# A fused attention, gated MLP and soft mixture-of-experts kernel: another tail, other slot logits, new step orders

## The chip, the cores and the metric

The kernel runs on one core of a Trainium2 chip. The metric is the device time of one launch in microseconds (us). In the words below PE is TensorE (PEld its weight loads), DVE is VectorE, ACT is ScalarE, POOL is GpSimd and SP is SyncE, whose queue issues nearly all DMAs. PSUM is the memory that PE writes its products to; DVE and ACT copy them out of it.

## What is computed

Three stages in a row, float32 in and out:

```python
# 1 attention: 4 batches, 12 heads, 448 rows, head width 64
q_n, k_n = rmsnorm(q, g_q), rmsnorm(k, g_k)
attn = softmax(q_n @ k_n.T / 8) @ v          # gathered to x: 1792 x 768
# 2 gated MLP: w_gate, w_val 768 x 1536, w_out 1536 x 768
x = (silu(x @ w_gate) * (x @ w_val)) @ w_out
# 3 soft mixture: phi 768 x 32, 8 experts with 4 slots each, w1 8 x 768 x 1024, w2 8 x 1024 x 768
logits = x @ phi                             # 1792 x 32
slot_input = softmax(logits, axis=0).T @ x   # 32 x 768
slot_out[e] = relu(slot_input[e] @ w1[e]) @ w2[e]
out = softmax(logits, axis=1) @ slot_out     # 1792 x 768
```

## The kernel before, in words

**Units of work.** The program is one long list of steps `t`, written out in Python. In the first 28 steps (`step0`, t below `M0`) PE does the attention of batch 0, one quarter of a head pair per step, and beside it the 12 blocks of `w_out` are multiplied with `phi` (tiles `wot`, `wpp`, `wpq`, `wp`). From t = 28 on (`step`) each step also multiplies one block of gate or value weights with a batch of `x` (`gv`, L615: 36 products of 128x128 by 128x448 into the tile `pg`); 24 such blocks make a batch, 96 all four. The attention of batches 1 to 3 runs beside them until t = 95. Weights and `x` are split in a rounded part and a rest (`wh`, `wl`, `xh`, `xl`; type fp32r) and multiplied in three terms.

**Orders.** Which piece of a step stands before which is set by lists of names: `ORDA`, `ORD0` and `ORDB` for t below 2, below 24 and below 28, `ORD1` for the batch 0 blocks and `ORD2` for the others. Every engine executes its own instructions in that order. Some of the names: `S` scores, `M0`/`M1` row maxima (DVE), `E0`/`E1` exponentials (ACT), `P0`/`P1` transposes of the probabilities (PE, tile `tp`), `V0`/`V1` their copies (tile `pt`), `X` probabilities times v, `T`/`TP` transposes of q and k, `G0`/`G1` the two halves of `gv`, `HT` transposes of the MLP's hidden rows (`th`), `LG` partial logits (`lp`), `NB` the transposed inverse sums (`rb`), `R` the integer part of a weight conversion (ACT or POOL, tiles `hpos`, `hneg`).

**Slots.** After a batch's 24 blocks come `Z1` to `Z4`. `slots1` sums the partial logits to `lt`, 128 x 448, each slot repeated four times, and multiplies the same logits once more into their transposed form `ln` (L703; in the last batch L705 too, since its last hidden block is not in the sum yet). `slots2` takes maximum and exponential and copies `ln` to `ce`, which the last stage's softmax over slots starts from. `slots3` transposes the exponentials (`dp`), DVE copies them to `dn`, and `slots4` multiplies the hidden rows with them (`sp`). In the last batch `slots4_last` adds the scaled sums of the other batches (`acl`, `wp`) and multiplies by `w_out` (`sip`).

**Experts and tail.** The expert weights (28 units of 1.5 MB) come through 15 buffers; a load is issued when the buffer's last reader is done. PE multiplies slots with w1 (L1431) and w2 (L1458, tile `so`, four column strips side by side). The last four units are the halves of the last two experts' w2, so that output columns 0 to 383 are ready before the others. `slot_out` (L1403 to L1407) then copies two 32-row strips of `so` into the zeroed tile `sos`, lays them over one another with a product by the 0/1 matrix `sel`, and splits that in rounded part and rest; `output` (L1417 to L1422) makes one 112 x 384 block of the output with one fp32r product of depth 96 from it and from `ct`, which holds the combine weights, their rest and the weights again. DVE and ACT copy the blocks out in turn and SP stores them in pairs. `TO` says how many of the 16 blocks of the first half stand after each of the last three units, `TF` and `LF` how many filler products (`fill`, L115, tile `warm_ps`) stand at given places.

Of the kernel before, what the change touches and what calls it, by code (L numbers as in the profile page):

```python
# [21 lines left out]
def attn_moe_softmoe_kernel(  # L22
# [15 lines left out]
    nc = tc.nc  # L38
# [649 lines left out]
    def slots1(b):  # L688

        d = bt[b]  # L690
        lg = d["lg"]
        d["lt"] = pt_tile("lt")
        n = NS * d["n"]
        ht = d["ht"].pop(KF - 1, None)
        one = ht is None
        nc.tensor.matmul(d["lt"][:, :S], stack[:n].rearrange("p j s -> p (j s)"), lg, start=True, stop=one)
        if not one:
            nc.tensor.matmul(d["lt"][:, :S], d["wp4"].rearrange("p j s -> p (j s)"), ht, start=False, stop=True)
            h_trans(B * NU - 1, ht)
        ln = pt_tile("ln")  # L700
        for c in range(NC):
            o, cs = ln[:CP, NS * c : NS * c + NS], slice(CP * c, CP * c + CP)
            nc.tensor.matmul(o, lg[:, cs], stack[:n, 0, :], start=True, stop=one)  # L703
            if not one:
                nc.tensor.matmul(o, ht[:, cs], wp[:, KF - 1, :], start=False, stop=True)  # L705
        d["ln"] = ln

    def slots2(b):
# [12 lines left out]
        nc.vector.tensor_copy(out=ce[:, b], in_=d.pop("ln")[:CP, : NC * NS].rearrange("p (c s) -> p c s", c=NC))  # L721
# [8 lines left out]
        d["et"] = et  # L730

    def slots3(b):
        d = bt[b]
        dp = pt_tile("dp")
        for c in range(NC):
            nc.tensor.transpose(
                dp[:CP, NS * c : NS * c + NS], d["et"][:NS, CP * c : CP * c + CP], ident[:NS, :NS]
            )
        d["dn"] = mp.tile([CP, NC, NS], F32, tag="dn", name="dn", bufs=1)
        nc.vector.tensor_copy(out=d["dn"], in_=dp[:CP, : NC * NS].rearrange("p (c s) -> p c s", c=NC))  # L740
# [75 lines left out]
    def acc_scale():  # L816
        accl.append(mp.tile([P, S], F32, tag="lg", name="acl", bufs=1))
        accl.append(wp.rearrange("p f s -> p (f s)"))
        accl.extend([ht_tile("acl", n) for n in (1, 0)])
        for g in range(NG):  # L820
            for r, o in acc_parts(g):
                nc.scalar.activation(out=o, in_=accp[g][:, r], func=AF.Copy, scale=bt[B - 1]["sml"][:, 3:4])
# [246 lines left out]
    def step(t):  # L1069
# [210 lines left out]
        "CT M0 M1 E0 E1 S X R P0 V0 P1 V1 NA NB TP TH SS WT WV U C WE NC XM U2 TL Q XH W2 XL G2"  # L1280
# [4 lines left out]
    ORDB = (  # L1285
        "M1 TP CT NA WT TH NB WV E1 M0 P1 P0 E0 X S R V1 U2 TL NC V0 U XM XH WE XL C G2 Q SS W2"
# [73 lines left out]
    with tc.manual_schedule():  # L1360
# [31 lines left out]
        sel = stack.rearrange("p j s -> p (j s)")[:, : 3 * NS]  # L1392
        sst = [None, None]

        def slot_out(n):

            if n == 0:
                t = unit_tile(NE + B).bitcast(F32R)
                sst[:] = [t[: 3 * NS, 384 * i : 384 * i + 384] for i in range(2)]
            r, cs = slice(2 * NS * n, 2 * NS * (n + 1)), slice(384 * n, 384 * n + 384)  # L1400
# [115 lines left out]
```

## Time and profile before

| what | us |
|---|---|
| median of 3 runs | 833.52 (832.75 to 835.16) |
| the profiled execution, own time | 833.85 |
| its span, first to last instruction | 832.1 |
| PE busy | 790.9 (95%) |
| DVE, ACT, POOL busy | 462.1, 439.3, 333.1 |

The page of the profile gives for each engine its busy time, and in 40 slices how busy it was and what TensorE clock was granted. The other views are answers of the same trace: busy times in chosen stretches, who waited for whom, the chain of waits that ended last in order of time, and the instructions in order of time. Matmuls are pipelined there and their ends are modelled, so the times of neighbours overlap.

### The profile page before, as it was taken

Reading aid. Unit: us, or ns where it says so; the run is one execution under the profiler, and the core shown is the slowest. Engines: PE = TensorE matmul, PEld = TensorE weight load, DVE = VectorE, ACT = ScalarE, POOL = GpSimd, SP = SyncE. Lnnn points to the kernel's source line nnn. Section 1 sums busy time; section 2 is a strip of 40 time slices with the busy share of each in tenths; the row PEclk is TensorE's granted clock in tenths of the full one; section 3 lists DMA queues with packets and bytes.
Section 4 is the critical chain, followed back from the end, with each engine's and each line's share of the span. In section 5 each row is a group of like instructions: output and inputs, shape, how many; then the busy total and the mean of one; then the engine's idle time right before and its main releaser. Section 6 shows DMA issues by size and latency. Waiting matters only on the chain.

```text
span 832.1 us, 14229 instructions
## 1 busy us (share of the span) xinstructions
PE 790.9 (95%) x5460; PEld 594.0 (71%) x5460; DVE 462.1 (56%) x777; ACT 439.3 (53%) x940; POOL 333.1 (40%) x327
## 2 busy tenths in 40 slices
PE   6799989999999999999999999999999999988685
PEld 5556657778778767787778677877878888555353
DVE  4879978777778555555556555545354344220013
ACT  3777877878678546556566455655333333220012
POOL 7987867675756543445444344322000000010000
PEclk8999999999999999999999999999999999999877
DMA  6566665765656312322223222221337778899997
GB/s 212 161 197 188 204 206 164 238 223 177 195 188 223 107 53 80 110 91 77 83 80 95 68 85 60 69 75 52 96 107 252 285 286 321 270 397 403 403 343 235
DMA packets 77891, 148.87 MB, mean 179 GB/s; under 512 B 5888, under 2 KB 48128, under 8 KB 77824
## 3 DMA queue, kind: packets, MB, share of 16 engines
q1 hardware_dynamic: 77824, 147.97, 53.5%
q8 instruction: 43, 0.70, 0.3%
q14 instruction: 24, 0.20, 0.1%
HBM read 128.29 MB, written 19.66 MB: 178 GB/s over the span
## 4 chain that ended last, share of the span: by engine, by line
PE 60%; DMA 6%; ACT 1%; POOL 1%; DVE 1%; issue 0%; SPq 0%; DVEq 0%; ACTq 0%; POOLq 0%
PE pg L615 33%; DMA w<-in_moe_w_dram 6%; PE tp L521 5%; PE xp L548 5%; PE s L442 3%; PE th L659 2%; PE so L1458 2%; PE sp L746 1%; PE lp L679 1%; PE tq L372 1%; PE s L446 1%; PE s L1417 1%; PE s L1431 1%; PE sip L800 0%; POOL pr L486 0%; PE ln L703 0%
## 5 line engine op out<-in xcount | busy, mean ns | idle before, releaser
L615 PE MATMUL pg<-xh,wh 128*128 128x448 f32 x576 | 222.5, 386 | 0.0
L615 PE MATMUL pg<-xl,wh 128*128 128x448 f32 x576 | 210.6, 366 | 0.0
L615 PE MATMUL pg<-xh,wl 128*128 128x448 f32 x432 | 157.9, 365 | 0.1
L457 DVE TENSOR_REDUCE sm<-s 128x1 f32<-128x448 f32 x168 | 100.5, 617 | 73.4 <-PE s L442 52.7
L469 ACT ACTIVATE pr<-s,sm 128x448 f32<-128x448 f32 x168 | 106.2, 639 | 63.5 <-DVE sm L457 61.1
L486 POOL TENSOR_SCALAR pr<-pr,su 128x448 f32<-128x448 f32 x84 | 70.9, 854 | 117.5 <-DVE su L482 106.0
L615 PEld LDWEIGHTS pg<-xh,wh 128*128 128x128 f32 x576 | 108.6, 189 | 12.4 <-issue 5.1
L615 PEld LDWEIGHTS pg<-xl,wh 128*128 128x128 f32 x576 | 108.9, 189 | 6.4
L521 PE MATMUL tp<-ident,pr 128*112 128x128 f32 x672 | 101.9, 280 | 4.3 <-ACT pt L535 2.1
L521 PEld LDWEIGHTS tp<-ident,pr 128*112 128x112 f32 x672 | 74.7, 135 | 38.2 <-issue 13.2
L231 ACT CAST wh<-raw 128x768 fp32r<-128x768 f32 x96 | 79.5, 830 | 29.0 <-PE pg L615 22.8
L239 DVE TENSOR_TENSOR wl<-raw,wh 128x768 fp32r<-128x768 f32 x72 | 81.0, 1124 | 11.2 <-ACT wh L231 11.2
L615 PEld LDWEIGHTS pg<-xh,wl 128*128 128x128 f32 x432 | 81.2, 188 | 7.2 <-DVE wl L239 0.5
L535 ACT COPY pt<-tp 112x512 f32<-112x512 f32 x130 | 74.0, 595 | 13.3 <-PE tp L521 7.4
L341 POOL TENSOR_TENSOR ri<-ss,mhalf 112x16 f32<-112x16 f32 (+1 forms) x25 | 70.1, 2805 | 2.1
L423 POOL CAST qz<-qa 64x128 fp32r<-64x128 f32 x48 | 35.1, 732 | 78.3 <-DVE qa L414 70.1
L442 PE MATMUL s<-ka,qa 64*128 64x448 f32 x432 | 63.6, 399 | 0.8 <-ACT qa L403 0.7
L660 ACT COPY hn<-th 112x512 f32<-112x512 f32 x48 | 28.4, 591 | 58.9 <-PE th L659 58.9
L548 PE MATMUL xp<-pt,vt 112*64 112x448 f32 x288 | 58.1, 546 | 0.0
L347 POOL TENSOR_TENSOR qn<-qk,ri 112x512 f32<-112x512 f32 x46 | 52.9, 1150 | 1.1
L615 PE MATMUL pg<-xh,raw 128*128 128x448 f32 x144 | 52.6, 366 | 0.0
L197 POOL TENSOR_SCALAR hpos<-r 128x768 uint16<-128x768 int16 x36 | 46.2, 1282 | 4.6 <-DMA r<-in_moe_w_gate_dram 1.7
(161 smaller groups left out, 1103.9 us busy)
## 6 DMA issues: line engine op xcount, KB each, us to landing
w<-in_moe_w_dram SPq DMA_DIRECT2D x25, 1536.0 KB, 10.6
raw<-w SPq DMA_DIRECT2D x72, 384.0 KB, 3.2
w<-raw SPq DMA_DIRECT2D x36, 384.0 KB, 2.9
r<-in_moe_w_out_dram SPq DMA_DIRECT2D x12, 768.0 KB, 5.1
r<-in_moe_w_gate_dram SPq DMA_DIRECT2D x12, 768.0 KB, 5.2
r<-in_moe_w_val_dram SPq DMA_DIRECT2D x12, 768.0 KB, 5.0
qk<-in_q_dram SPq DMA_DIRECT2D x24, 224.0 KB, 3.2
qk<-in_k_dram SPq DMA_DIRECT2D x24, 224.0 KB, 3.4
```

The costliest lines, as they stand in the source:

```text
L231: (nc.vector.tensor_copy if u - NO < NU and WH1 == "v" else nc.scalar.copy)(out=wh, in_=wst[u]["raw"])
L239: eng.tensor_tensor(out=wl, in0=wst[u]["raw"], in1=wst[u]["wh"].bitcast(F32), op=ALU.subtract)
L341: nc.gpsimd.tensor_tensor(out=ri, in0=ss, in1=mhalf[:, : len(ns)], op=ALU.pow)
L347: eng.tensor_tensor(out=st[i]["qn"][:, n].rearrange("p c h d -> p h c d"), in0=st[i]["qk"][:, n], in1=st[i]["ri"][:, n] .rearrange("p (h c ...
L442: nc.tensor.matmul(sc[j], qa[r, wt, c * P : (c + 1) * P], ka[r, mv, :], start=(n == 0), stop=(n == 2))
L457: nc.vector.tensor_reduce(out=d["sm"][:, j : j + 1], in_=d["sc"][j], axis=AX.X, op=ALU.max, negate=True)
L469: nc.scalar.activation(out=p, in_=d["sc"][j], func=AF.Exp, bias=d["sm"][:, j : j + 1], accum_out=st[i]["su"][:, c, j : j + 1])
L486: nc.gpsimd.tensor_scalar(out=p, in0=p, scalar1=su[:, j : j + 1], scalar2=1.0, op0=ALU.mult, op1=ALU.mult)
L521: nc.tensor.transpose(tp[:CP, ck * P : (ck + 1) * P], pr[:, ck * CP : (ck + 1) * CP], ident)
L535: eng(out=st[i]["pt"][j][:, :, c * P : (c + 1) * P], in_=tp)
L548: nc.tensor.matmul(xp[HD * j : HD * j + HD, :S], d["vt"][:, j, ck, :], d["pt"][j][:, ck, :], start=(ck == 0), stop=(ck == NC - 1),)
L615: nc.tensor.matmul(d[r], wt[:, P * c : P * c + P], mv, start=(c == 0 and n == 0), stop=(c == KD - 1 and n == 2),)
```

## The change

Five things change.

1. `slots1` no longer makes `ln`. `slots2` copies the first 32 rows of `lt` to `lr` (the space of `lg`), and `slots3` transposes `lr` beside the exponentials and copies it to `ce`, on DVE, in the last batch on ACT.
2. In the last batch the 12 filler products ahead of `slots1` go (`LF`, in fours), and the sums are kept in other tiles (`accl`).
3. The tail's products are in full float32, of depth 32: `ct` holds four equal copies of the combine weights, one for each strip of rows, `slot_out` is one copy of 64 rows, and a block takes two products of 192 columns, one from each strip, into two PSUM tiles; DVE copies the first, ACT the second. `sel`, the split and the zeroing are gone.
4. `TO` puts all 16 blocks of the first half ahead of the products of the last two units, and `TF` (in fours too) drops the tail's fillers, 16 products in each of two places.
5. All five order lists are new.

```diff
@@ slots1
-        ln = pt_tile("ln")
-        for c in range(NC):
-            o, cs = ln[:CP, NS * c : NS * c + NS], slice(CP * c, CP * c + CP)
-            nc.tensor.matmul(o, lg[:, cs], stack[:n, 0, :], start=True, stop=one)
-            if not one:
-                nc.tensor.matmul(o, ht[:, cs], wp[:, KF - 1, :], start=False, stop=True)
-        d["ln"] = ln
@@ slots2
-        nc.vector.tensor_copy(out=ce[:, b], in_=d.pop("ln")[:CP, : NC * NS].rearrange("p (c s) -> p c s", c=NC))
...
+        d["lr"] = d["lg"][:NS]
+        (nc.vector.tensor_copy if LRE == "v" else nc.scalar.copy)(out=d["lr"], in_=lt[:NS, :S])
@@ slots3
+        for n, (src, dst) in enumerate(((d["et"], d["dn"]), (d["lr"], ce[:, b]))):
+            o = dp[:CP, NC * NS * n : NC * NS * (n + 1)]
+            for c in range(NC):
+                nc.tensor.transpose(o[:, NS * c : NS * c + NS], src[:NS, CP * c : CP * c + CP], ident[:NS, :NS])
+            if n == 0 or b < B - 1:
+                nc.vector.tensor_copy(out=dst, in_=o.rearrange("p (c s) -> p c s", c=NC))
+            else:
+                nc.scalar.copy(out=dst, in_=o.rearrange("p (c s) -> p c s", c=NC))
@@ combine2, combine3: four copies of the weights for three, one ACT copy for ACT's cast and DVE's rest
-        cb = ct[:, S * b : S * b + S]
-        evac_hi(cb, cp[: 3 * NS, :S])
-        sub_lo(cb[NS : 2 * NS], cp[NS : 2 * NS, :S], cb[NS : 2 * NS])
+        nc.scalar.copy(out=ct[:, S * b : S * b + S], in_=cp[:, :S])
@@ the lists (ORD1, ORD2, ORDA and ORDB are new in the same way)
-    LF = [4, 3, 2, 3]
+    LF = [4, 3, 2, 0]
+    LRE = 'v'
-    TF, TO = [0, 0, 0, 0, 4, 4, 0], [0, 8, 16, 16]
+    TF, TO = [0, 0, 0, 0, 0, 0, 0], [0, 16, 16, 16]
-        "M1 X TP M0 P0 R NA SS WT NB TH S U2 TL V0 WV P1 NC XM U CT C W2 XH E0 E1 V1 WE Q XL G2"
+        "X TP P0 M0 WT NB M1 R SS TH NA V0 S U2 P1 NC XM U WV CT TL E0 XH C V1 XL W2 G2 E1 Q WE"
@@ slot_out
-            for j in (2 * n, 2 * n + 1):
-                eng = nc.scalar.copy if j % 2 else nc.vector.tensor_copy
-                eng(out=sos[NS * j : NS * j + NS, DQ * j : DQ * j + DQ], in_=so[NS * j : NS * j + NS, :])
-            s3 = pt_tile("s3")
-            nc.tensor.matmul(s3[: 3 * NS, :384], sel[r], sos[r, cs], start=True, stop=True)
             fill(TF[5 + n])
-            nc.scalar.copy(out=sst[n], in_=s3[: 3 * NS, :384])
-            sub_lo(sst[n][2 * NS :], s3[2 * NS : 3 * NS, :384], sst[n][2 * NS :])
+            (nc.scalar.copy if n else nc.vector.tensor_copy)(out=sos[r], in_=so[r, :])
@@ output
-            op = (s_tile(i % 5) if i % 5 < 3 else pt_tile("op"))[:CP, :384]
-            nc.tensor.matmul(op, ct[:, S * b + CP * c : S * b + CP * c + CP], sst[n], start=True, stop=True)
-            eng = nc.scalar.copy if c % 2 else nc.vector.tensor_copy
-            eng(out=ot[b][:, c, cs], in_=op)
+            ops = [(s_tile(k) if k < 3 else pt_tile("op"))[:CP, :DQ] for k in ((2 * i + j) % 6 for j in range(2))]
+            for j in range(2):
+                r = slice(NS * (2 * n + j), NS * (2 * n + j + 1))
+                nc.tensor.matmul(
+                    ops[j], ct[r, S * b + CP * c : S * b + CP * c + CP], sos[r], start=True, stop=True
+                )
+            for j, eng in enumerate((nc.vector.tensor_copy, nc.scalar.copy)):
+                eng(out=ot[b][:, c, DQ * (2 * n + j) : DQ * (2 * n + j + 1)], in_=ops[j])
```

How the instructions stand at three places follows; a row is line, operation, output and inputs, and size.

PE in the tail before, from the eighth output block to the products of the last unit (`s` and `op` are blocks of the output, by the PSUM tile that they go to):

```order
L1417 MATMUL s<-w,ct 112x384 x3
L1458 MATMUL so<-w,h1m 32x192 x16
L1417 MATMUL op<-w,ct 112x384 x2
L1417 MATMUL s<-w,ct 112x384 x3
L1417 MATMUL op<-w,ct 112x384 x2
L1417 MATMUL s<-w,ct 112x384
L1458 MATMUL so<-w,h1m 32x192 x16
```

and PE of the change, the end of the same stretch:

```order
L1404 MATMUL s<-sos,ct 112x192 x3
L1404 MATMUL op<-sos,ct 112x192 x3
L1404 MATMUL s<-sos,ct 112x192 x2
L1447 MATMUL so<-w,h1m 32x192 x32
L1404 MATMUL s<-sos,ct 112x192 x3
```

The products of the last two units (`so`, two times 16) moved behind the whole first half, whose 16 blocks are now 32 products of half the width.

DVE in the last batch's slots before, from the maximum of `lt` to the first sum for `sip`:

```order
L716 TENSOR_REDUCE sml<-lt 128x1
L720 TENSOR_TENSOR mrun<-mrun,sml 128x1
L721 COPY ce<-ln 112x128
L727 SCALAR_TENSOR_TENSOR ssum<-ssum,sml 128x1
L740 COPY dn<-dp 112x128
L784 TENSOR_TENSOR acl<-acl,sp 128x384
```

and in the change:

```order
L709 TENSOR_REDUCE sml<-lt 128x1
L713 TENSOR_TENSOR mrun<-mrun,sml 128x1
L719 SCALAR_TENSOR_TENSOR ssum<-ssum,sml 128x1
L724 COPY lg<-lt 32x448
L736 COPY dn<-dp 112x128
L782 TENSOR_TENSOR wp<-wp,sp 128x384
```

The copy from `ln` ahead of `ssum` is gone, and a copy of 32x448 logits stands ahead of the copy to `dn` instead.

PE at the slots of the second batch before (`pg` is `G0`, one row of its nine shown at each end):

```order
L736 MATMUL dp<-ident,et 112x32 x4
L521 MATMUL tp<-ident,pr 112x128 x4
L615 MATMUL pg<-xh,wh 128x448
...
L615 MATMUL pg<-xh,wl 128x448
L746 MATMUL sp<-hn,dn 32x512 x12
```

and in the change:

```order
L442 MATMUL s<-ka,qa 128x448 x6
L734 MATMUL dp<-ident,et 112x32 x4
L734 MATMUL dp<-ident,lg 112x32 x4
L744 MATMUL sp<-hn,dn 32x512 x12
L521 MATMUL tp<-ident,pr 112x128 x4
```

The `sp` products, which read DVE's copy `dn` of the first transposes, stood behind nine `pg` products and now follow the transposes directly. Over the whole list PE's `pg` products, cut in 137 runs before, are cut in 160: 23 of the runs of 18 became two runs of 9 with transposes between them, and 19 of the 23 runs of 8 `tp` transposes became two of 4.

## Rows read from the trace of the kernel before

**Rows 1.** Busy us by stretch (PE, PEld, DVE, ACT, POOL), granted clock, DMA share, GB/s.

```profile
125.00:700.00 575.00, 574.35 (x3360) 454.85 (x3358) 338.70 (x550) 328.68 (x673) 227.98 (x215) 1.00 0.42 138
740.00:780.00 40.00, 34.03 (x622) 20.46 (x614) 5.55 (x18) 4.11 (x10) 4.02 (x11) 1.00 1.03 403
```

**Rows 2.** Waits of PE, 20 to 130 us: total us, times, longest.

```profile
PE tp L521 <- ACT pt L535: 2.1, 1, 2.1
...
PE rb L505 <- ACT pt L535: 1.3, 1, 1.3
...
PE warm_ps L115 <- ACT pr L469: 0.2, 1, 0.2
```

**Rows 3.** Busy us as in rows 1, 12 to 48 us.

```profile
12.00:48.00 36.00, 26.88 (x197) 18.39 (x198) 24.30 (x39) 22.20 (x54) 33.83 (x33) 0.91 0.61 189
```

**Rows 4.** Chain of waits in order of time: start us, us, what; around 280 us.

```profile
276.75 1.06 PE tp L521 x8
277.81 3.67 PE pg L615 x18
...
288.24 0.58 PE tp L521 x4
288.82 1.84 PE pg L615 x9
290.65 0.44 PE th L659 x4
```

**Rows 5.** Chain of waits, slots of the third and the last batch.

```profile
613.66 0.75 PE lt L696 x2
614.41 0.72 PE ln L703 x8
...
617.04 0.33 PE dp L736 x4
...
711.92 0.69 PE warm_ps L115 x12
```

**Rows 6.** Instructions in order of time: start, us, [idle before]; last batch's slots.

```profile
708.12 0.61 DVE L685 TENSOR_TENSOR lg<-lp,lg 32x448 f32<-32x448 f32 x1 [3.33 <-PE lp L679]
...
715.46 0.64 ACT L724 ACTIVATE et<-lt,mrun 128x448 f32<-128x448 f32 x1
...
718.46 0.29 DVE L740 COPY dn<-dp 112x128 f32<-112x128 f32 x1 [0.58 <-PE dp L736]
...
719.23 4.08 PE L746 MATMUL sp<-hn,dn 112*32 112x512 f32 x24
```

**Rows 7.** Waits of SP's queue, 715 to 740 us.

```profile
SPq L906 <- PE sp L746: 10.2, 2, 8.9
```

**Rows 8.** Instructions in order of time, tail.

```profile
804.22 0.34 DVE L1403 COPY sos<-so 32x192 f32<-32x192 f32 x1 [6.93 <-PE so L1458]
...
808.10 19.58 SPq L1422 DMA_DIRECT2D out_dram<-w  x18
...
813.57 2.79 PE L1458 MATMUL so<-w,h1m 128*32 128x192 f32 x32
...
819.33 0.78 PE L1417 MATMUL s<-w,ct 96*112 96x384 f32 x3 [1.15 <-DVE w L62]
...
819.80 1.02 DVE L1419 COPY w<-s 112x384 f32<-112x384 f32 x2 [0.52 <-PE s L1417]
```

**Rows 9.** Busy us as in rows 1; around the last slots and in the tail.

```profile
720.00:722.00 2.00, 2.00 (x16) 0.57 (x12) 0.69 (x2) 0.00 (x0) 0.00 (x0) 0.53 0.12 40
...
807.00:809.00 2.00, 1.95 (x10) 1.29 (x12) 1.48 (x4) 1.26 (x3) 0.00 (x0) 1.00 0.47 165
809.00:818.00 9.00, 9.00 (x91) 5.96 (x90) 2.77 (x7) 2.56 (x7) 0.00 (x0) 1.00 0.96 293
818.00:821.00 3.00, 1.85 (x9) 1.20 (x8) 1.76 (x4) 1.46 (x4) 0.00 (x0) 0.98 0.12 42
821.00:830.00 9.00, 3.10 (x10) 2.45 (x9) 2.97 (x6) 2.74 (x6) 0.00 (x0) 0.50 0.95 294
```

More of the change, by code (lines that the diff above doesn't have):

```diff
@@ L734, in slots3 @@
         dp = pt_tile("dp")
[L735 to L738, printed above, removed]
         d["dn"] = mp.tile([CP, NC, NS], F32, tag="dn", name="dn", bufs=1)
-        nc.vector.tensor_copy(out=d["dn"], in_=dp[:CP, : NC * NS].rearrange("p (c s) -> p c s", c=NC))
+        for n, (src, dst) in enumerate(((d["et"], d["dn"]), (d["lr"], ce[:, b]))):
[6 more added lines that the diff above has]
+                nc.scalar.copy(out=dst, in_=o.rearrange("p (c s) -> p c s", c=NC))
     def slots4_mul(b, g):
@@ L816, in acc_scale @@
     def acc_scale():
-        accl.append(mp.tile([P, S], F32, tag="lg", name="acl", bufs=1))
         accl.append(wp.rearrange("p f s -> p (f s)"))
         accl.extend([ht_tile("acl", n) for n in (1, 0)])
+        accl.append(mp.tile([P, S], F32, tag="lg", name="acl", bufs=1))
         for g in range(NG):
@@ L841, in combine2 @@
     def combine2(pool, b):
-        c3s[b] = pool.tile([CP, NC, 3, NS], F32, tag="c3", name="c3", bufs=2)
-        nc.gpsimd.tensor_copy(out=c3s[b], in_=ce[:, b].unsqueeze(2).to_broadcast([CP, NC, 3, NS]))
+        c3s[b] = pool.tile([CP, NC, 4, NS], F32, tag="c3", name="c3", bufs=2)
+        nc.gpsimd.tensor_copy(out=c3s[b], in_=ce[:, b].unsqueeze(2).to_broadcast([CP, NC, 4, NS]))
     def combine3(b, ct):
@@ L1279, in attn_moe_softmoe_kernel @@
     ORDA = (
-        "CT M0 M1 E0 E1 S X R P0 V0 P1 V1 NA NB TP TH SS WT WV U C WE NC XM U2 TL Q XH W2 XL G2"
+        "U2 U WT M0 M1 E1 P0 R CT E0 X NB TP V0 WE P1 TH W2 WV Q V1 NC TL SS NA C XM XH S G2 XL"
     ).split()
     ORD0 = (
-        "M1 X TP M0 P0 R NA SS WT NB TH S U2 TL V0 WV P1 NC XM U CT C W2 XH E0 E1 V1 WE Q XL G2"
+        "X TP P0 M0 WT NB M1 R SS TH NA V0 S U2 P1 NC XM U WV CT TL E0 XH C V1 XL W2 G2 E1 Q WE"
     ).split()
     ORDB = (
-        "M1 TP CT NA WT TH NB WV E1 M0 P1 P0 E0 X S R V1 U2 TL NC V0 U XM XH WE XL C G2 Q SS W2"
+        "WT M1 TP M0 X TH NB P0 NA TL WV CT NC E1 XM E0 P1 U2 V1 U S R V0 W2 WE XH C XL G2 SS Q"
     ).split()
@@ L1383, in attn_moe_softmoe_kernel @@
         warm_tag[0] = "v"
-        ct = tp_.tile([3 * NS, NT], F32R, name="ct")
-        sos = tp_.tile([P, DM], F32, tag="si", name="sos")
-        nc.gpsimd.memset(sos, 0.0)
+        ct = tp_.tile([P, NT], F32, name="ct")
+        sos = tp_.tile([P, DM // 4], F32, name="sos")
         so = ps.tile([P, 192], F32, tag="g", name="so")
@@ L1391, in attn_moe_softmoe_kernel @@
         ot = {}
-        sel = stack.rearrange("p j s -> p (j s)")[:, : 3 * NS]
-        sst = [None, None]
         def slot_out(n):
[L1397 to L1400, printed above, removed]
-            for j in (2 * n, 2 * n + 1):
-                eng = nc.scalar.copy if j % 2 else nc.vector.tensor_copy
-                eng(out=sos[NS * j : NS * j + NS, DQ * j : DQ * j + DQ], in_=so[NS * j : NS * j + NS, :])
-            s3 = pt_tile("s3")
-            nc.tensor.matmul(s3[: 3 * NS, :384], sel[r], sos[r, cs], start=True, stop=True)
+            r = slice(2 * NS * n, 2 * NS * (n + 1))
             fill(TF[5 + n])
-            nc.scalar.copy(out=sst[n], in_=s3[: 3 * NS, :384])
-            sub_lo(sst[n][2 * NS :], s3[2 * NS : 3 * NS, :384], sst[n][2 * NS :])
+            (nc.scalar.copy if n else nc.vector.tensor_copy)(out=sos[r], in_=so[r, :])
         def output(n, i):
```

6 lines of the change are left out of this document (3 added, 3 removed).

## The prediction

> **What bounds the kernel now.** The busy times by stretch come first. From 125 to 700 us PE is busy 574.35 of 575 us at full clock while DVE and ACT have 59% and the DMA engines 42% [rows 1]: there the time is PE's own work, and only fewer or cheaper PE instructions, or a new wait, can move it. From 740 to 780 us the picture turns over: the DMA engines are full (1.03, 403 GB/s) with the expert weights, and PE has slack [rows 1]; that stretch moves only as a whole, by when its loads begin. Ahead of 125 us PE waits now and then; nine waits from 2.1 down to 0.2 us add up to 8.2 us [rows 2]. Behind 804 us the stretches of rows 9 show the output stores: full from 809 to 818 and from 821 to 830 us, nearly idle in between.
>
> A bound is therefore read per stage, and the stages follow each other: PE's list sets when buffers come free, that sets the loads, the loads set the last products, and those the stores. A gain on PE ahead of 718 us passes on in full, since SP waits for PE there (10.2 us in two waits for the `sp` products) [rows 7].
>
> I work against the profiled execution, 833.85 us (span 832.1); it lies 0.33 above the median of 833.52. A measurement of this kernel tells about 0.3% from no change, 2.5 us.
>
> **The start, to 125 us: -1.0.** The new lists change here what DVE and ACT do first; PE keeps its order from the third step to the 24th. From 12 to 48 us POOL is busy 33.83 of 36 us [rows 3] and its order is unchanged, so what PE gains there it waits for again at the next POOL result; the waits of that stretch stay. Behind it the visible waits are 1.3 us (`rb` for ACT's copies, in a step where a weight conversion stood ahead of them on ACT; the new `ORDB` puts one copy ahead), 0.5 and 0.4. So at best 2.2 us go. The other side: `ORDA` and `ORDB` put the scores at the end of six steps, and each maximum could come later by the six products of a group, 1.2 us at the 0.2 of a product in rows 4, 7 us in all, though PE has other products to do meanwhile. Within -2.2 and +7 I take -1.0, nearer to the waits that rows show.
>
> **PE's list, 125 to 711 us: -1.1.** Three parts.
>
> *Slots of the first three batches.* `ln` is 0.72 us of PE and goes; the transposes `dp` are 0.33 and double [rows 5]. That is 0.39 less, three times, -1.2. The copy to `lr` takes about 0.61 on DVE, by the same shape in rows 6; nine `pg` products at least, 1.84 us, cover it [rows 4]; without that cover it would be 0.6 us in each batch. Now `sp` stands right behind the transposes. DVE's copy to `dn` takes 0.29 [rows 6] and needs the first four transposes; the other four, 0.33, just cover it, but not the handovers, nor anything that DVE has ahead of it. I count 0.25 of waiting for each batch, +0.8 (0 to 0.6, a copy like `lr` ahead, for each). Together -0.4.
>
> *More, shorter runs.* 23 runs of 18 `pg` products become two of 9 with transposes between. Eight transposes and 18 products took 1.06 + 3.67 = 4.73; four, nine, four, nine take 2 x (0.58 + 1.84) = 4.84 if both groups of four are as dear as one behind scores, and 0.58 + 0.44 + 2 x 1.84 = 4.70 if the second costs what four transposes cost between products [rows 4]. So 23 x -0.03 to 23 x +0.11: -0.7 to +2.5. In the new lists the second group does stand between products, so -0.7.
>
> *Waits.* PE's queue shows no idle to speak of here, and DVE and ACT are at 57 to 59%. A new order can still make a PSUM bank late: `P1` in `ORD2` now takes the bank that `XL` empties in the steps with `X`. By the durations of that step the bank is free at about the moment PE comes to it; 0, and up to 0.1 us in each of 40 steps (+4) for the range.
>
> **The last batch's slots, and the gap in the loads: -1.8.** The chain from the last `pg` product to `sp`: the 12 fillers at 711.92 stand first and leave, 0.69 us [rows 5], so that the exponential starts at 714.8 in place of 715.46 [rows 6]. DVE then waited with everything until `ln` was done. Now the two exponentials are done some 0.9 later (715.7), the update of the sum 0.2 (715.9), `lr` 0.61 (716.5), `dn` 0.29 plus starts (716.9); PE transposes `lr` meanwhile, runs eight fillers and begins `sp` at 717.4, not 719.23 [rows 6]. SP was waiting for those products [rows 7], and the DMA engines ran dry: share 0.12 from 720 to 722 us [rows 9], 1.76 us lost. With the loads issued 1.8 us earlier this gap closes. I count no more, since loads ahead of the gap stay behind the same `pg` products. If `sp` also ran at full clock (it took 4.08 us with the clock at 0.53), PE would be earlier still, but the loads could not use it. If the clock fell longer in the idle moments that now stand before `dp`, 1.3 us of the 1.8 would go.
>
> ACT's extra copy, 0.29 if as long as DVE's, stands ahead of its scalings of the sums; it hides behind `sp`, whose first third takes longer than that. The larger copies of the combine weights (POOL, ACT) lie in the stretch where DMA is full [rows 1] and cost nothing; without that cover, under 1 us.
>
> **The tail: -3.5.** `so` of the first half is complete at 804.2. Before, the first store was issued at 808.10 [rows 8]. Now one copy (0.34 for a strip of the same width) ends at 804.6 and products begin.
>
> *Price of a block on PE.* 32 `so` instructions of 192 columns took 2.79 us [rows 8], 0.087 each, while `lt`, two of 448 columns alone in the array, took 0.75 [rows 5], or 0.16 for 192 columns: strips run two at a time, and one float32 product is two instructions. A block is four instructions: 0.33 us if the two 32-row strips run side by side as the column strips do, 0.64 if not. I take 0.33, the nearer row. DVE takes 0.51 for 384 columns and 0.34 for 192 [rows 8], ACT copies beside it; six PSUM tiles hold three blocks. So 0.37 per block.
>
> *First half.* 16 blocks end at 804.6 + 5.9 = 810.5. The stores, 16 x 112 x 384 x 4 bytes = 2.75 MB, go at 293 GB/s [rows 9], 9.4 us, behind the last weights, which half of 807 to 809 still shows (say until 807.5): to 816.9. Meanwhile PE does the last two units, 2 x 2.72: 816.0.
>
> *Second half.* Copy and first block: the first store at 817.2, where it was about 820.5; 9.4 us at the same rate give 826.6 for 830.3. So -3.7, and I take -3.5 for a late block or two. What I recover are the idle 2.6 us of 818 to 821 and the 1.06 of 807 to 809 [rows 9]; with every other share below 1 counted too the bound is -4.5. The other bound is in the rivals.
>
> **Sum.** -1.0 - 1.1 - 1.8 - 3.5 = -7.4: 826.45 for a profiled execution like this one, 826.1 by the median; I say **826.0**.
>
> **Rivals.**
>
> *The clock drops in the tail.* The granted clock was 0.50 from 821 to 830 [rows 9], behind an idle of 1.15 us on PE [rows 8], although fillers stood before it; the change takes the fillers out. At the lower of the two levels, 1.2 GHz, a block of the second half costs 0.66 and 16 cost 10.6: from 816.4 to 827.0, and the last store lands 2.4 later (336 KB at 293 GB/s is 1.2, as much again for issue and landing, an estimate), near 829.4 for 830.3. Then the tail gives only -0.9: 829.0 (15%). For it: 32 filler products gone. Against: the idle between `so` and the first block shrinks from over 1.15 to about 0.45, and the products are denser. The Trainium skill (TensorE: Matmul & The Clock Gate, "Part 1: The HAM clock gate") has the array at half rate unless recent activity lifts it, which speaks against dropping fillers; by it alone the sum would be this rival's, and the row shows that fillers alone did not hold the clock either.
>
> *The new orders cost waits on PE.* A PSUM bank or a copy comes late in many steps of 125 to 711 us: +4 by the bound above, 830.0 (13%). For it: five lists change at once, and shorter runs give more places to wait. Against: 574.35 of 575.
>
> *The new orders save more.* The waits ahead of 125 us shrink further or transposes get cheaper everywhere: 4 us more, 822.0 (14%).
>
> *Strips of rows do not run side by side,* so that PE, not the stores, paces the tail. A block then costs 0.64 at full clock: 10.2 for the first half, 814.8; last units, 820.3; second half from 820.7 to 830.9; last store landed and closed about 835.1, where the span ended at 832.1, +3.0 for -3.5: 832.6. At the lower clock in the second half 1.28 a block: +10.2 more, 842.8, slower. The price of a block decides: 32 blocks pay, so each 0.1 us is 3.2 us. The tail gains nothing at 0.54, the whole change at 0.66, and it is slower by over 0.3% from 0.74 on. For it: the trace of before has float32 column strips, and rows of 64 only in fp32r, so that 32-row strips in float32 are shown by no row. Against: scores of two row halves overlap there. 8%, half of it at the lower clock. The Trainium skill (TensorEngine Tiling (Array Packing), "Key Properties") says that different tiles can load weights and multiply in parallel; no run here shows it for these.
>
> **How the numbers follow.** Forecast 50%, the rivals 15, 13, 14 and 8. From 821.5 (a bit beyond the saving rival) to 832.0 the range holds the forecast, the first three rivals and most of their spread. Faster than 831.0: nearly all of the forecast (0.48), most of the clock rival (0.12), half of the costly orders (0.07), the saving orders (0.14), 0.81. Slower than 836.0: the half of the last rival at the lower clock and a little of the second, 0.06. Between: 0.13.
>
> **What would show it.** In the profile after: no `ln`; PE idle in 125 to 700 under 2 us; DMA share from 720 to 722 shifted with the whole and near 1; the first store within 1.5 us of the first half's last `so` product; 16 blocks in about 6 us each; no gap in the stores over 1 us between the halves; the end 24.4 us behind the first half's last `so` product, where it was 27.9 (832.1 - 804.2). It is wrong if blocks take 0.6 us or more, if PE shows waits for DVE or ACT in the middle, or if the gap in the loads is still there.

## The result and the profile after

The changed kernel takes **826.64 us** (median of 4 runs, 825.36 to 827.47), the one before 833.93 beside it: a ratio of 0.991, with a 95% interval of 0.9894 to 0.9927. The profiled execution took 826.44, its span is 824.5 against 832.1. The forecast was 826.0.

The span falls into four stretches that follow each other: the start, to the first block product `pg`; the blocks, to the start of the last `pg` product; from there to the first half's last `so` product (read at the copy that waits for it); and the tail. The figures are rounded one by one.

| us | start | blocks | last block to first half | tail | span |
|---|---|---|---|---|---|
| before | 125.9 | 585.6 | 92.7 | 27.8 | 832.1 |
| after | 124.7 | 583.7 | 91.5 | 24.5 | 824.5 |
| difference | -1.2 | -1.9 | -1.2 | -3.3 | -7.6 |
| predicted | -1.0 | -1.1 | -1.8 | -3.5 | -7.4 |

The waits of PE at the start, 20 to 127 us, and then those of 125 to 730 us (total us, times, longest) answer to [rows 2]:

```profile
PE rb L505 <- POOL rs L494: 1.5, 1, 1.5
PE tw L247 <- DVE raw L212: 1.3, 2, 0.8
...
PE tp L521 <- ACT pt L535: 0.7, 1, 0.7
```

```profile
PE dp L734 <- DVE dn L736: 2.5, 4, 0.8
...
PE dp L734 <- ACT et L716: 0.6, 1, 0.6
```

Before, of the same stretches:

```profile
PE tw L247 <- ACT pt L535: 0.7, 1, 0.7
...
PE tw L247 <- ACT pt L537: 0.4, 1, 0.4
```

```profile
PE tp L521 <- POOL pr L486: 0.5, 1, 0.5
```

The wait of `rb` for ACT's copies is gone, as said. `tw` waits 1.3 for DVE, at the same two places where it waited 1.1 for ACT before. `tp` behind ACT's `pt` shrank from 2.1 to 0.7. Among the blocks the wait of 0.5 for POOL is gone and one is new: the second slot transposes for DVE's `dn`, 0.39, 0.75 and 0.63 in the first three batches. A fourth one of 0.76, and the 0.6 for `et`, stand in the last batch's slots, behind the blocks.

The last batch's slots in order of time (start, us, [idle before]) answer to [rows 6]:

```profile
711.66 0.64 ACT L716 ACTIVATE et<-lt,mrun 128x448 f32<-128x448 f32 x1
...
712.45 0.40 PE L734 MATMUL dp<-ident,et 32*112 32x32 f32 x4 [0.63 <-ACT et L716]
712.61 0.22 DVE L719 SCALAR_TENSOR_TENSOR ssum<-ssum,sml 128x1 f32<-128x1 f32 x1 [1.05 <-ACT sml L718]
712.75 0.60 DVE L724 COPY lg<-lt 32x448 f32<-32x448 f32 x1
713.28 0.27 DVE L736 COPY dn<-dp 112x128 f32<-112x128 f32 x1
713.60 0.40 PE L734 MATMUL dp<-ident,lg 32*112 32x32 f32 x4 [0.76 <-DVE dn L736]
...
714.49 2.78 PE L744 MATMUL sp<-hn,dn 112*32 112x512 f32 x24
...
725.98 1.52 PE L1374 MATMUL sit<-stack,si 128*128 128x32 f32 x12
```

The last `pg` starts at 708.45, so `sp` stands 6.04 behind it, 7.67 before (719.23 - 711.56): 1.6 earlier. It also ran at full clock, 2.78 for 4.08. `sit` is the transposed slot input that the first expert products read; its first product starts 17.5 behind the last `pg`, 20.5 before. The stretches of busy time (PE, PEld, DVE, ACT, POOL, then granted clock, DMA share, GB/s) answer to [rows 1, 9]:

```profile
125.00:700.00 575.00, 573.21 (x3352) 453.12 (x3352) 329.96 (x552) 328.53 (x670) 234.78 (x215) 1.00 0.43 140
...
714.00:716.00 2.00, 2.00 (x25) 0.93 (x28) 0.31 (x1) 1.96 (x7) 0.00 (x0) 1.00 1.03 414
718.00:720.00 2.00, 1.65 (x19) 0.58 (x18) 0.39 (x3) 0.27 (x1) 0.00 (x0) 1.00 1.06 323
...
716.50:728.50 12.00, 10.36 (x104) 5.94 (x100) 2.09 (x7) 1.95 (x6) 0.31 (x1) 1.00 0.95 312
...
801.00:810.00 9.00, 9.00 (x110) 6.74 (x108) 5.35 (x16) 5.08 (x16) 0.00 (x0) 1.00 1.02 341
...
812.00:814.00 2.00, 2.00 (x26) 1.70 (x26) 1.59 (x5) 1.49 (x5) 0.00 (x0) 1.00 0.19 54
814.00:822.00 8.00, 3.49 (x42) 2.56 (x39) 3.81 (x12) 3.60 (x12) 0.00 (x0) 0.96 0.98 302
```

The hole in the loads (0.12 of the DMA's time from 720 to 722 us before) is closed: 1.03 and 1.06 around `sp`. That is no return to 403 GB/s: in the 12 us from 8 us behind the last `pg` on, the loads move 312 GB/s, where it was 273 before:

```profile
719.60:731.60 12.00, 10.94 (x96) 4.86 (x88) 2.48 (x8) 1.00 (x4) 0.00 (x0) 0.90 0.79 273
```

In the tail the first half's stores, with the last loads among them at first, run at 341 GB/s, are done early, and leave a hole at 812 to 814. The tail in order of time answers to [rows 8]:

```profile
799.94 0.35 DVE L1393 COPY sos<-so 64x192 f32<-64x192 f32 x1 [8.49 <-PE so L1447]
800.34 0.74 PE L1404 MATMUL s<-sos,ct 32*112 32x192 f32 x5 [0.44 <-DVE sos L1393]
...
801.38 0.84 SPq L1411 DMA_DIRECT2D out_dram<-w  x2
...
805.98 5.39 PE L1447 MATMUL so<-w,h1m 128*32 128x192 f32 x64
...
811.42 0.31 ACT L1393 COPY sos<-so 64x192 f32<-64x192 f32 x1 [4.98 <-PE so L1447]
811.78 0.74 PE L1404 MATMUL s<-sos,ct 32*112 32x192 f32 x5 [0.41 <-ACT sos L1393]
```

16 blocks take 5.64 us (800.34 to 805.98), 0.35 each. From the first half to the first product of the second it was 804.22 to 819.33, 15.11 us, and is 799.94 to 811.78, 11.84: the whole 3.3. Behind that product both kernels take the same, 12.7.

### The profile page after: what moved, and what is told of

Read it like the earlier page. It is cut to its first block, busy times and chain, and to the rows that moved or that the text cites. A ratio compares the mean times of both kernels' runs of the same rounds, so it can differ in the third digit from the quotient of the medians.

```text
span 824.5 us, 14367 instructions
## 1 busy us (share of the span) xinstructions
PE 781.6 (95%) x5484; PEld 589.2 (71%) x5484; DVE 455.5 (55%) x789; ACT 441.2 (54%) x954; POOL 341.4 (41%) x326
## 4 chain that ended last, share of the span: by engine, by line
PE 85%; DMA 6%; POOL 3%; ACT 2%; DVE 2%; issue 1%; SPq 0%; POOLq 0%; ACTq 0%; DVEq 0%
PE pg L615 42%; PE tp L521 9%; PE xp L548 7%; PE s L442 6%; DMA w<-in_moe_w_dram 6%; PE tq L372 3%; PE th L659 3%; PE s L548 2%; PE so L1447 2%; PE s L446 2%; PE lp L679 2%; PE sp L744 1%; PE s L1420 1%; PE s L1404 1%; PE tw L247 1%
## 5 line engine op out<-in xcount | busy, mean ns | idle before, releaser
L486 POOL TENSOR_SCALAR pr<-pr,su 128x448 f32<-128x448 f32 x84 | 80.4, 967 | 139.9 <-ACT pt L535 62.5
L521 PE MATMUL tp<-ident,pr 128*112 128x128 f32 x672 | 103.6, 277 | 1.5 <-ACT pr L469 0.7
L239 DVE TENSOR_TENSOR wl<-raw,wh 128x768 fp32r<-128x768 f32 x72 | 74.4, 1034 | 8.3 <-ACT wh L231 8.3
L341 POOL TENSOR_TENSOR ri<-ss,mhalf 112x16 f32<-112x16 f32 (+1 forms) x25 | 72.8, 2912 | 2.1
L347 POOL TENSOR_TENSOR qn<-qk,ri 112x512 f32<-112x512 f32 x46 | 59.1, 1286 | 1.1
L1430 POOL MEMSET h1m<- 128x256 f32 x8 | 2.5, 311 | 129.6 <-ACT acl L820 98.1
L442 PEld LDWEIGHTS s<-ka,qa 64*128 64x128 f32 x432 | 35.5, 187 | 27.6 <-issue 24.4
L629 ACT ACTIVATE ht<-pg 128x448 f32<-128x448 f32 x48 | 26.1, 544 | 46.0 <-PE pg L615 29.8
```

The source lines that it names most:

```text
L239: eng.tensor_tensor(out=wl, in0=wst[u]["raw"], in1=wst[u]["wh"].bitcast(F32), op=ALU.subtract)
L341: nc.gpsimd.tensor_tensor(out=ri, in0=ss, in1=mhalf[:, : len(ns)], op=ALU.pow)
L347: eng.tensor_tensor(out=st[i]["qn"][:, n].rearrange("p c h d -> p h c d"), in0=st[i]["qk"][:, n], in1=st[i]["ri"][:, n] .rearrange("p (h c ...
L442: nc.tensor.matmul(sc[j], qa[r, wt, c * P : (c + 1) * P], ka[r, mv, :], start=(n == 0), stop=(n == 2))
L486: nc.gpsimd.tensor_scalar(out=p, in0=p, scalar1=su[:, j : j + 1], scalar2=1.0, op0=ALU.mult, op1=ALU.mult)
L521: nc.tensor.transpose(tp[:CP, ck * P : (ck + 1) * P], pr[:, ck * CP : (ck + 1) * CP], ident)
```

## The experiments

**Three parts undone, one at a time, and one taken apart;** the kernel before has 834.27 beside them.

Lists of before:

```diff
     ORD2 = (
-        "X S NB Z3 T AT NC M0 AM XM XH TH W4 M1 Z4 XL P0 V0 E0 L SP WH G0 NA Z1 CT E1 HT N0 R0 Z2 N1 N2 SS P1 G1 WL R LG V1 Q C"
+        "T S AT TH M0 Z3 NB X NC P0 AM XM XH W4 M1 XL SP CT E0 SS NA G0 E1 Z1 WH V0 N0 Z4 P1 Q HT L R0 N2 V1 N1 C Z2 WL R G1 LG"
...
```

> The changed kernel with the five lists of before; slots, tail and placement as changed. Theory: the new orders alone bring the gain ahead of the last slots, about 3 us by the two traces (1.2 to the first block at 125 us and 1.9 from there to the last block), so the time is 829.6 and the last block's first product starts near 711.5 in the profile. The prediction had 1.0 + 0.7 for the orders, which gives 828.3. Rival: the gain of that stretch comes from the slots without the transposed logits and not from the lists; then 827 or less, and the last block starts near 708.5 as in the changed kernel.

Measured: **832.67**, ratio to before 0.9978 (0.9967 to 0.9988), 6 us slower than the changed kernel, twice what the theory gave. The blocks take 588.8 us, 5.1 more than in the changed kernel and 3.1 more than in the kernel *before*. 2.6 of these 3.1 lie at the second batch's slots, here in order of time:

```profile
467.89 0.40 PE L734 MATMUL dp<-ident,et 32*112 32x32 f32 x4
468.07 0.93 DVE L239 TENSOR_TENSOR wl<-raw,wh 128x768 fp32r<-128x768 f32 x1
468.93 0.60 DVE L457 TENSOR_REDUCE sm<-s 128x1 f32<-128x448 f32 x1
469.47 0.27 DVE L736 COPY dn<-dp 112x128 f32<-112x128 f32 x1
469.79 0.40 PE L734 MATMUL dp<-ident,lg 32*112 32x32 f32 x4 [1.50 <-DVE dn L736]
```

and the stretch of busy time behind it:

```profile
471.00:474.00 3.00, 3.00 (x12) 2.19 (x15) 0.92 (x4) 1.93 (x4) 1.06 (x2) 0.50 0.41 150
```

In the old order a weight rest (`wl`) and a row maximum (`sm`) stand on DVE ahead of `dn`. PE stands still for 1.5 us, and behind that the granted clock is 0.50, its lower level, for some 3 us. The wait and the clock together make the place 2.6 dearer than it was before. The rival falls, as the last block's last product starts at 714.5: the gain of that stretch is bound to the lists.

Slots of before (`ln`, its copy, 12 fillers, the sums' tiles):

```diff
-    LF = [4, 3, 2, 0]
+    LF = [4, 3, 2, 3]
...
+        ln = pt_tile("ln")
...
```

> The changed kernel with the slots of before (transposed logits by their own products, their copy, the 12 fillers in the last batch, the sums in the tiles of before); lists and tail as changed. Theory: the last batch's slots bring 1.6 (the sp products begin that much later again and the DMA engines run dry near 720 us for about 1.8 us), the slots of the first three batches next to nothing, so 828.3, and the clock is granted at half around the sp products. Rival 1: the first three batches pay too, 0.39 each, 829.4. Rival 2: the gap in the loads was only moved, not closed, and the loads wait for other buffers anyway: 826.6.

Measured: **828.37**, 0.9926 (0.9909 to 0.9943, or 826.7 to 829.5 us), the theory's time. `sp` begins 7.76 behind the last `pg`, the waits of SP's queue are those of [rows 7] again, and the loads run dry, at a clock of 0.66, in the waits and by stretch:

```profile
SPq L904 <- PE sp L746: 10.1, 2, 9.0
```

```profile
718.00:720.00 2.00, 2.00 (x20) 0.43 (x12) 0.75 (x2) 0.00 (x0) 0.00 (x0) 0.66 0.04 6
```

The blocks take 584.3, 0.6 more: 0.4 in the first batch's slots, 0.2 in the third's, nothing in the second's. The second rival falls, as the hole in the loads is back. The first is half right: 0.6 lies between the theory's next to nothing and its 1.2, and the interval of the time holds both.

Tail of before (fp32r products of depth 96, `sel`, split, 8 and 8 blocks, fillers):

```diff
-    TF, TO = [0, 0, 0, 0, 0, 0, 0], [0, 16, 16, 16]
+    TF, TO = [0, 0, 0, 0, 4, 4, 0], [0, 8, 16, 16]
...
```

> The changed kernel with the tail of before (fp32r products of depth 96 with the selecting product, split and zeroing, 8 first-half blocks ahead of each of the last two units, 32 fillers); lists and slots as changed. Theory: the tail brings 3.3 between the first half's last so product and the end, so 829.9; from that product to the end 27.9 us as before, with two gaps in the stores of together about 3.5 us. Rival: half of what the tail seemed to bring is the clock, which was at its lower level from 783 to 800 us and from 821 us in the profile of before and at its higher one throughout in the changed kernel; if that comes from the work ahead of the tail and not from the tail, then the clock stays high here as well and the time is about 828.2.

Measured: **829.14**, 0.9945 (0.993 to 0.996). From the first half's last `so` to the end 27.8 us, as before. The clock stayed at full through the old tail's second half, 816 to 820:

```profile
814.00:816.00 2.00, 1.79 (x8) 1.31 (x9) 1.48 (x4) 1.10 (x3) 0.00 (x0) 1.00 0.01 3
816.00:820.00 4.00, 2.04 (x9) 1.16 (x8) 2.48 (x6) 2.41 (x6) 0.00 (x0) 1.00 0.98 298
```

and the tail was no shorter for it: in the old tail the second half's stores take the same time at either clock. So the rival's reason falls. Up to the tail this is the changed kernel's program, yet `sp` ran at the lower clock here:

```profile
714.04 4.48 PE L744 MATMUL sp<-hn,dn 112*32 112x512 f32 x24
...
727.24 1.52 PE L1376 MATMUL sit<-stack,si 128*128 128x32 f32 x12
```

The time itself, 2.5 over the changed kernel, lies between the two (829.9 and 828.2) and doesn't decide.

Products of full depth:

```diff
-            (nc.scalar.copy if n else nc.vector.tensor_copy)(out=sos[r], in_=so[r, :])
+            for j, eng in ((2 * n, nc.vector.tensor_copy), (2 * n + 1, nc.scalar.copy)):
+                eng(out=sos[NS * j : NS * j + NS, j], in_=so[NS * j : NS * j + NS, :])
...
-                    ops[j], ct[r, S * b + CP * c : S * b + CP * c + CP], sos[r], start=True, stop=True
+                    ops[j], ct[:, S * b + CP * c : S * b + CP * c + CP], sos[:, 2 * n + j], start=True, stop=True
```

> The changed kernel with output products of depth 128 instead of 32: each strip of 32 rows is copied into a tile that is zero in the other rows, and the product takes all 128 rows, so that two products can't stand in the array side by side; result, number and width of the products, PSUM tiles and copies out stay. Theory (two strips of rows run side by side in the changed kernel): a block costs 0.64 on PE in place of 0.34, 16 blocks 10.2 us for 5.6; PE paces the tail: first half done near 810.6, last units 816, second half 826.6, end 2.5 us later, so about 831.0. Rival (the strips do not run side by side, and a product of 192 columns just costs 0.17): no change on PE, 826.6.

Measured: **833.56**, 0.9997 (0.9985 to 1.0009): all of the gain is gone. PE in order of time:

```profile
798.03 1.30 PE L1405 MATMUL s<-sos,ct 128*112 128x192 f32 x6 [0.44 <-DVE sos L1395]
799.17 1.14 PE L1405 MATMUL op<-sos,ct 128*112 128x192 f32 x6
...
807.94 0.81 PE L1405 MATMUL s<-sos,ct 128*112 128x192 f32 x4
808.69 5.39 PE L1448 MATMUL so<-w,h1m 128*32 128x192 f32 x64
```

16 blocks take 10.66 us, 0.67 each in place of 0.35, with the same count and width of products. In the changed kernel the products of the two strips start in pairs (800.92 both), the next pair 0.16 later:

```profile
800.92 0.32 PE L1404 MATMUL s<-sos,ct 32*112 32x192 f32 x1
800.92 0.65 PE L1404 MATMUL op<-sos,ct 32*112 32x192 f32 x5
```

Of full depth one starts alone every 0.16 us. So two strips of 32 rows do multiply side by side, and the rival falls: it is not the smaller depth that makes a product cheaper. The tail is 32.3 us, 7.7 longer, more than the theory's 4.4: PE now paces both halves, each with 5.0 us more of products.

**A second set,** with 834.66 for the kernel before. That kernel with the new tail alone:

```diff
-            s3 = pt_tile("s3")
-            nc.tensor.matmul(s3[: 3 * NS, :384], sel[r], sos[r, cs], start=True, stop=True)
...
+            (nc.scalar.copy if n else nc.vector.tensor_copy)(out=sos[r], in_=so[r, :])
...
```

> The kernel before with nothing but the new tail (products of depth 32, one copy, 16 blocks ahead of the last two units, no fillers there); slots and lists of before. It completes the square of slots and lists, all with the new tail: new slots with new lists 826.6, new slots with old lists 832.7, old slots with new lists 828.4. Theory (slots and lists depend on each other: the new slots make PE wait wherever the old lists leave DVE no time, and cost 2 us there): about 830.7 (3.3 less than before), so the new slots are worth -1.7 with the new lists and +2 with the old. Rival (they add up: the lists are worth 6 with either slots): 834.4, and the tail alone gives nothing against the kernel before.

Measured: **829.53**, 0.9947 (0.9926 to 0.9967). The square, all with the new tail:

| | lists before | lists new |
|---|---|---|
| slots before | 829.5; blocks 585.6 | 828.4; blocks 584.3 |
| slots new | 832.7; blocks 588.8 | 826.6; blocks 583.7 |

The two at the lower left and upper right are from the first set. With the old lists the new slots cost 3.1, with the new lists they save 1.7; by the ratios, which take out the difference between the sets, 2.6 and 1.3. The intervals of the cost's two runs no more than touch, those of the saving's overlap. The rival (they add up, 834.4) falls.

A PSUM tile of its own for the second slot transposes:

```diff
-            o = dp[:CP, NC * NS * n : NC * NS * (n + 1)]
+            o = (pt_tile("dp") if n else dp)[:CP, : NC * NS]
```

> The changed kernel with the second group of slot transposes (those of the logits) written to a PSUM tile of its own instead of the second half of the first group's tile. In the changed kernel that group waits, four times, 2.5 us in all, for DVE's copy dn of the first group, though it reads nothing that the copy writes. Theory (the wait is for the tile, which DVE still reads): the waits ahead of the second group go, PE then waits a little for dn ahead of sp (0 to 0.2 each time, as the four transposes of 0.33 stand in between); 0.4 less in each of the first three batches, 0.5 to 0.7 less in the last, so about 825.0. Rival (the group waits for the copy lr, or DVE's count, which the tile doesn't change): no change, 826.6. Second rival: the extra PSUM tile shifts the banks of the others and costs a wait in the middle: 828 or more.

Measured: **825.76**, 0.9894 (0.9874 to 0.9914). The first batch's slots in order of time:

```profile
302.95 0.40 PE L734 MATMUL dp<-ident,et 32*112 32x32 f32 x4
303.19 0.38 PE L734 MATMUL dp<-ident,lg 32*112 32x32 f32 x4
...
303.39 0.29 DVE L736 COPY dn<-dp 112x128 f32<-112x128 f32 x1 [0.19 <-PE dp L734]
...
303.74 1.50 PE L744 MATMUL sp<-hn,dn 112*32 112x512 f32 x12 [0.17 <-DVE dn L736]
```

The second transposes follow the first at once; in the changed kernel they began 0.78 behind (301.45, 302.23). So they waited for the tile that DVE was still reading, and what is left here is a wait of 0.17 ahead of `sp`. In the other batches more is left, since DVE's copies themselves come late: 0.54 ahead of `sp` for `dn`, behind a weight rest, in the second, and 0.53 and 0.65 ahead of the second transposes for the copy `lr` in the third and the last:

```profile
466.77 1.92 PE L744 MATMUL sp<-hn,dn 112*32 112x512 f32 x16 [0.54 <-DVE dn L736]
...
614.71 0.37 PE L734 MATMUL dp<-ident,lg 32*112 32x32 f32 x4 [0.53 <-DVE lg L724]
```

The blocks take 582.9, 0.8 less. In time the interval overlaps that of the changed kernel; the gain is shown in the trace only.

In a third set, with 834.07 for before, the copy `lr` on ACT on top of it:

```diff
-    LRE = 'v'
+    LRE = 'a'
```

> The run with two tiles for the slot transposes, and the copy lr on ACT instead of DVE. There, in the third and the last batch, the second transposes wait 0.53 and 0.65 us for DVE's copy lr, which also stands ahead of DVE's copy dn. Theory: with lr on ACT both go together (DVE copies dn while ACT copies lr), 0.3 to 0.5 less in each of these two batches, nothing in the others: 0.6 to 1.0 less than with two tiles alone, 825.0 where that had 825.8, a ratio to the changed kernel of 0.998. Rival: ACT's copy of 0.6 comes as late as DVE's, or delays ACT's copies of the probabilities by which PE goes on: no gain or 1 us lost, 825.8 to 827.

Measured: **825.20**, 0.9889 (0.9867 to 0.991); the changed kernel itself again beside it:

> The changed kernel as it is, beside the run before on the same chip, so that the two can be told apart to about 0.2%: 826.6 by all that is known; the start, to the first block, 124.2 to 126.3 (its spread in the profiles with the new lists), the blocks 583.7 from first to last.

Measured: **826.49**, 0.9908 (0.9889 to 0.9927). With both edits the blocks take 582.3, 1.4 less than in the changed kernel and 0.6 less than with two tiles alone, and `sp` begins 5.47 behind the last `pg`, 0.6 and 0.4 sooner: in the trace the theory's 1.0. It is the fastest of the versions by its median, but not told apart from the changed kernel: in its profile the stretch behind the last block was 91.6 where the repeat of the changed kernel had 89.8, and took the gain back. Why that stretch differs is not settled (below).

Placement of before in the new tail:

```diff
-    TF, TO = [0, 0, 0, 0, 0, 0, 0], [0, 16, 16, 16]
+    TF, TO = [0, 0, 0, 0, 0, 0, 0], [0, 8, 16, 16]
```

> The changed kernel with the placement of before: 8 blocks of the first half ahead of each of the last two units instead of 16 ahead of both. Theory (stores pace the first half and only the second half's start counts, which the order of blocks and units on PE does not change): 8 blocks are 1.38 MB, 4.1 us of stores at 340 GB/s, and 2.8 us pass on PE before the next ones, so the stores never run dry for more than a few tenths in the first half; the same 826.6. Rival (all blocks first matter, as the prediction's sum took it, with the stores running dry between the two groups): up to 1.5 us slower, 828.1.

Measured: **825.99**, 0.9893 (0.9874 to 0.9912), the tail 24.8 us. As the theory had it, placing all blocks first is worth nothing: the hole between the stores is divided, not larger:

```profile
806.00:808.00 2.00, 2.00 (x26) 1.64 (x24) 1.98 (x6) 1.88 (x6) 0.00 (x0) 1.00 0.68 224
...
812.00:814.00 2.00, 2.00 (x28) 1.64 (x26) 1.89 (x6) 1.78 (x6) 0.00 (x0) 1.00 0.39 118
```

The three lists of the first 28 steps of before:

```diff
     ORD0 = (
-        "X TP P0 M0 WT NB M1 R SS TH NA V0 S U2 P1 NC XM U WV CT TL E0 XH C V1 XL W2 G2 E1 Q WE"
+        "M1 X TP M0 P0 R NA SS WT NB TH S U2 TL V0 WV P1 NC XM U CT C W2 XH E0 E1 V1 WE Q XL G2"
...
```

> The changed kernel with ORDA, ORD0 and ORDB of before (the first 28 steps), ORD1 and ORD2 as changed. Theory: these three lists bring 1.7 us between the first scores and the first block (113.3 in the profiles with the old lists, 111.5 to 112.0 with the new ones), and the first sixteenth of the blocks is decided by ORD1: 41.2 as in the changed kernel, not 42.4. So the first block starts 113.3 behind the first scores and the whole takes 828.3. Rival: the waits at 96 to 125 us come from what ORD1 does ahead of them: first block 111.6 behind the first scores and 826.6.

One execution: 827.20, the first block at 126.6, 113.8 behind the first scores; the blocks 584.1, so that 1.5 of the 1.9 there come from ORD1, ORD2 and the slots. For the start the theory fits, but two kernels of the same set with the new first lists, those with two tiles and with the placement of before, had 113.4 and 113.0. The traces settle why. From the step near 43 us where `rb` waits for POOL to the first block it is 82.4 us in all four profiles with the old first lists, 81.5 in six of the eight with the new ones, and 83.0 in those two. The busy time just behind that wait of 1.5 us, in the changed kernel and then with two tiles:

```profile
45.00:47.00 2.00, 2.00 (x21) 0.92 (x21) 1.48 (x4) 1.68 (x4) 1.83 (x3) 1.00 0.00 0
```

```profile
45.00:47.00 2.00, 2.00 (x18) 1.26 (x16) 0.58 (x1) 1.65 (x4) 1.84 (x3) 0.50 0.00 0
```

The granted clock was 0.50 with two tiles, and with the placement of before too, and that costs 1.5. So behind 43 us the new first lists bring 0.9, and the lower clock behind the same wait takes it back in some executions.

## Why the prediction was right, point by point

Single profiles scatter, so means over all of them: start 126.0 with the old first lists (four profiles, 125.7 to 126.6), 124.9 with the new (eight, 124.2 to 126.2): -1.1. Last block to first half 92.2 with the old slots (three, 91.4 to 92.7), 90.6 with the new (nine, 89.7 to 91.8): -1.7. Tail 27.84 (two) and 24.9 (nine, without the products of full depth): -2.9. With the blocks' -1.9 that is -7.6. That the sum came so near is in part luck: in the changed kernel's profile the blocks gave 0.8 more than said and the last slots 0.6 less.

- **What bounds each stage** held: each stage's gain reached the end, and 740 to 780 us kept its 403 GB/s.
- **Start, -1.0:** the size held by the means, the way in part. The `rb` wait of 1.3 went as said, and 0.9 of it stayed, 82.4 to 81.5 from 43 us to the first block; in two profiles the lower clock took it back. Ahead of 43 us, where nothing was to change since POOL is full, the way from the first scores to that `rb` was 30.5 to 31.4 with the old lists and is 30.1 to 30.5, about 0.7 less by the means. There `tp` waits for ACT's `pt`: 2.1 to 2.9 with the old lists, 0.5 to 1.8 with the new.
- **Blocks, -1.1:** -1.9. Batch 0's blocks, with no slots among them, got 1.7 shorter. A block is 18 products, not the 36 of the description (the trace has 1728 for 96 blocks), and among batch 0's 432 stood 24 runs of 18 before and 1 after, so all 23 split runs lie there. But "23 x -0.03" is not what was too small. Of the 1.7, 0.4 lie within the first block, most of it ahead of the third product, 0.5 behind the second before and 0.2 now (the run with the first lists of before has these 0.4 again); 0.5 are `tp`'s wait for POOL near 268 us, which the new lists don't have. That leaves 0.8 for 23 split runs, 0.035 each. Too small was the term for waits, put at nothing, though two went (and the slots' came, below). The slots were -0.6 for the -0.4 given; in the other three batches the new lists cost 0.4 (old slots, old against new lists).
- **Waits in the blocks:** the wait was put at `sp`, behind `dn`, with the second transposes as its cover; it came ahead of those transposes, which share the first ones' tile, so that nothing covered the copy. Nor did the `pg` products cover the copy `lr` in the third batch, where it stands on DVE right ahead of `dn` (0.53 in the run with two tiles). "PE shows waits for DVE or ACT in the middle" was given as a sign of being wrong, and this part was: 1.8 us of such waits stand there. What the sum missed is that slots and lists are one change: with the old lists the slots would have cost 3.
- **Last slots and loads, -1.8:** -1.2 in the changed kernel's profile, -1.7 by the means. `sp` came 1.6 sooner and the hole of the loads closed, as said. Of what `sp` would save by its clock the prediction said that "the loads could not use it", and that step did not hold. The first product of `sit` begins 20.4 to 20.5 us behind the last `pg` with the old slots and `sp` at the lower clock, 18.8 with the old slots and `sp` at full clock, 19.1 to 19.2 with the new slots and `sp` at the lower clock, 17.0 to 17.5 with the new slots at full clock. From `sit` to the first half's last `so` it is 71.8 to 72.7 us in ten of the twelve profiles: the stretch follows `sit`, and with it the clock of `sp`. The two exceptions are the changed kernel's first profile, 74.0, and the last version's, 74.7. The other seven profiles with the new slots are shorter than 92.7 by 2.7 to 3.0 (five) or, with `sp` at the lower clock, by 0.9 to 1.6 (two), so that -1.8 met no single case.
- **Tail, -3.5:** -3.3, and -2.9 by the means. A block costs 0.35 on PE for the 0.33 taken. Wrong was the rate of the first half's stores, 341 for 293 GB/s, and so "no gap over 1 us between the halves": 812 to 814 has a share of 0.19. It did not matter, as the second half's start on PE sets the end. The step that was overrated is the placement, worth nothing; of the 3.3, 2.6 are the shorter way from the second half's last `so` to its first product (813.57 + 2.79 to 819.33, 2.97 us, before [rows 8]; 0.41 now).
- **The clock rival** did not come: in all ten profiles without the tail's fillers the clock stayed at full up to the last product, though the kernel of the old lists and the starts of two others show that an idle of 1.5 us can lower it. The Trainium skill (TensorE: Matmul & The Clock Gate, "Part 1: The HAM clock gate") ties the rate to recent activity; the trace agrees in both places.
- **The slower rival,** strips not side by side, is what the products of full depth built: 833.6 by measurement, 832.6 in the rival's sum. It fell for the changed kernel, at 0.35 against its break-even of 0.66. The Trainium skill (TensorEngine Tiling (Array Packing), "Key Properties") has tiles multiply in parallel, and the runs now show it for strips of 32 rows in float32.

Open: why the stretch behind the last block was about 2 us longer in two profiles (the changed kernel's first and the last version's) than its `sit` accounts for, and why the clock falls behind the same wait in some executions and not in others; no run was aimed at either.

## What to carry to other kernels

Price a shorter piece of work together with the order that it stands in: the same edit saved 1 to 2 us or cost 3, by what stood on DVE ahead of one copy. Two results that one engine writes and another copies out one after the other want two PSUM tiles, or the second write waits for the first copy (0.1 to 0.4 us a batch here). When a saving is credited to many small places, take out the single waits that came and went first. When profiles differ by 1.5 us over a stretch in which their programs are the same, look at the granted clock behind each wait. Small products of few rows should stand in different row strips in turn, and where blocks of output are stored in two halves, the way from the last product to the second half's first block is what counts, not where the first half's blocks are put.

## What was not expected of the hardware

A wait of 1.5 us on PE can be followed by the lower clock. With the lists of before the granted clock was 0.50 for some 3 us from about 1 us behind the end of such a wait (471 to 474 us), and the place cost 2.6. At the start the wait of 1.5 for POOL was followed by 0.50 in two of eight profiles, which cost 1.5 each, and by full clock in the other six. Two products of depth 32 and 192 columns take 0.35 together, two of depth 128 take 0.67. The DMA engines moved 403 GB/s of loads, 341 of stores in the first half, mixed at first with loads, and 302 in the second.
